# Half of the second group's w_in part by 20 products, and the sums of w_in moved to GpSimd

## The chip, the cores and the metric

The kernel runs on one core of a Trainium2 chip. The metric is the device time of one execution in microseconds (us); lower is better. The core has five engines with a queue each: TensorE (matmul; PE in the profile, and PEld for its weight loads), VectorE (DVE), ScalarE (ACT), GpSimd (POOL) and SyncE (SP, which issues most of the DMAs here).

## The reference

```python
def _attn_ref(q, k, v, alpha):                      # (4, 8, 768, 48) each
    for t in range(S):
        state = alpha[:, :, t, :, None] * state + einsum('bhd,bhe->bhde', k[:, :, t], v[:, :, t])
        y[:, :, t] = einsum('bhd,bhde->bhe', q[:, :, t], state)
def _moe_ref(x, w_in, w_out):                       # x (3072, 384), w_in (384, 2048), w_out (2048, 384)
    h = x @ w_in
    g = h * (1.0 / (1.0 + exp(-h)))
    return g @ w_out
```

A gated linear recurrence over 768 steps, for 4 batches of 8 heads of width 48, gives 3072 rows of 384 numbers (x). They go through a matrix of 384 x 2048 (w_in), the silu function, and a matrix of 2048 x 384 (w_out).

## The kernel before

The rows are cut into 24 chunks of 128 tokens. The recurrence of a chunk is done in stages spread over the steps of the main loop (from line 1357): products and quotient (L766, L795: scans on VectorE), scores (L834: matmuls, copies by ScalarE and a causal select by GpSimd, L860 for the first 8 chunks and L872 after them), values and states (L898, L924). Between the stages the loop puts pieces of the two big matrix products, as filler for TensorE.

Four chunks make a group, so there are 6 groups (grp 0 to 5). A group's 512 rows are two halves h of 256 columns in `xt`. The 2048 columns of w_in are cut into two pairs (pair 0 and 1) of 1024, and a pair into 2 tiles of 4 x 128 columns. A group's work on w_in can be done in two ways:

- `enter_plain(grp, h, pair)` (L971): 4 pieces, each 2 x 3 matmuls of 128x128 weights by 256 columns, and one silu by ScalarE (L983). A group and pair need it for both h: 8 pieces, 48 matmuls.
- `enter(grp, pair)` (L991): a fast matrix multiplication with 20 products in place of 24, each for the 2 tiles of the pair: 7 pieces, 40 matmuls. It needs sums of blocks of x (`sums_x`, L950, 11 sums, in the tile `xc`) and sums of blocks of w_in (`sums_w`, L608, 23 sums for each pair, in the tile `wx` and over blocks of w_in itself, so that plain work on that pair can't follow). It evicts its PSUM banks by copies of ScalarE (L1010) and additions and subtractions of VectorE (L1018), before four silus by ScalarE (L1015).

All sums are made by `combine` on VectorE (L599 to L606): an addition, a subtraction, or, where both signs are negative, one scalar_tensor_tensor. In `SUMS_W` two of the 23 have both signs negative (the 10th and the 17th).

`leave(grp, h)` (L1111) is the work on w_out for half a group: 7 pieces, one product of 8 matmuls each, after a scheme with 7 products in place of 8. Between them VectorE subtracts cells of g (L1123), and the four results are copied (L1130) or added (L1132) into `o` (3 buffers) and stored by a DMA on GpSimd's queue (L1135). After each piece `done()` (L1140) issues up to four sums of w_in: those of pair 0 in leave(0, 1), those of pair 1 in leave(1, 0).

The order of the pieces is written out by hand (L1225 to L1244): plain work for all of group 0 and for (grp 1, h 0, pair 0); leave(0, 0); plain (1, 1, 0); then leave(0, 1) interleaved piece by piece with the plain work of group 1 on pair 1; then leave(1, 0) with enter(2, 0), leave(1, 1) with enter(2, 1), and so on. Each piece has a weight of 12 (0 for sums of x), and `fill` (L1275) issues pieces so that a phase is done by its mark. `settle` (L1262) runs once in between: it closes the staging pools of the first phase, makes the later tiles (`xc` and `wx` among them), clears three load buffers by GpSimd memsets (L1272) and loads chunk 8.

The queue of an engine is filled by a scheduler, in the order in which instructions come ready. `tc.keep_in_program_order` pins an instruction behind the one traced before it on its engine; all sums of w_in are pinned.

Of the kernel before, what the change touches and what calls it, by code (L numbers as in the profile page):

```python
# [356 lines left out]
def quotients(  # L357
# [61 lines left out]
    def pool(name, bufs=1, space=None):  # L419
        kw = {} if space is None else {"space": space}  # L420
        return ctx.enter_context(tc.tile_pool(name=name, bufs=bufs, **kw))
# [169 lines left out]

    quads = w_in.rearrange("p k (q i c) -> p i k q c", i=4, c=128)

    def block_w(at):

        return quads[:, at // NKT, at % NKT] if at < 4 * NKT else late["wx"][:, at - 4 * NKT]


    def combine(to, sa, a, sb, b):  # L599
        if sa == sb == 1:  # L600
            return dve.tensor_tensor(to, a, b, ALU.add)
        if sa == 1:
            return dve.tensor_tensor(to, a, b, ALU.subtract)
        if sb == 1:
            return dve.tensor_tensor(to, b, a, ALU.subtract)
        return dve.scalar_tensor_tensor(to, a, -1.0, b, ALU.mult, ALU.subtract)  # L606

    def sums_w(pair, upto):  # L608

        r = slice(2 * pair, 2 * pair + 2)  # L610
        while sums_done[pair] < min(upto, len(SUMS_W)):
            to, sa, a, sb, b = SUMS_W[sums_done[pair]]
            tc.keep_in_program_order(
                combine(block_w(to)[:, r], sa, block_w(a)[:, r], sb, block_w(b)[:, r]))
            sums_done[pair] += 1

    sums_done = [0] * (NQ // 2)
# [326 lines left out]
    def block_x(grp, at):  # L944

        if at < 2 * NKT:
            return xts[2 * grp + at % 2][:, at // 2, :]
        return xcs[grp][:, at - 2 * NKT, :]

    def sums_x(grp):  # L950
        xcs[grp] = late["xc"]
        for i, (to, sa, a, sb, b) in enumerate(SUMS_X):
            if i == 2:
                yield
            tc.keep_in_program_order(
                combine(block_x(grp, to), sa, block_x(grp, a), sb, block_x(grp, b)))
        yield
# [33 lines left out]
    def enter(grp, pair):  # L991
        g_tiles(grp, pair)
        halves = [gts[grp, h, pair] for h in range(2)]

        s = [halves[o % 2][:, o // 2] for o in range(8)]
        todo = iter(PRODUCTS)

        def new(i):
            return bank(i).rearrange("p (e n) -> p e n", e=2)

        def add(ps, first=False):
            w, x = next(todo)
            for e in range(2):
                pe.matmul(ps[:, e], lhsT=block_w(w)[:, 2 * pair + e], rhs=block_x(grp, x),
                          start=(first and e == 0), stop=(e == 1), skip_group_check=True)

        def copy(ps, to=None):
            if to is None:
                to = late["part"].tile([128, 2, TB], F32, name="part")
            act.copy(to, ps)  # L1010
            return to

        def silu(h, i):
            x = halves[h][:, i : i + 2]
            return act.activation(x, x, AF.Silu)  # L1015

        def tt(to, a, b, op=ALU.add):
            dve.tensor_tensor(to, a, b, op)  # L1018

        a, b, c = [new(i) for i in range(3)]  # L1020
        add(a, True)
        copy(a, s[6])
        add(b, True)
        copy(b, s[2])
        add(c, True)
        tt(s[6], s[6], copy(c), ALU.subtract)
        yield
        add(c)
        copy(c, s[7])
        add(b)  # L1030
        copy(b, s[4])
        add(a)
        tt(s[7], s[7], copy(a), ALU.subtract)
        yield
        add(a)
        copy(a, s[5])
        add(b)
        copy(b, s[3])
        tt(s[5], s[5], s[3])
        add(c)  # L1040
        copy(c, s[0])
        yield
        add(a)
        tt(s[4], a, s[4])
        b = new(1)
        add(b, True)
        add(b)
        copy(b, s[1])
        yield
        c = new(2)  # L1050
        add(c, True)
        t = copy(c)
        late_2 = (grp, pair) == (4, 0)
        if not late_2:
# [12 lines left out]
        yield  # L1067
        add(c)
        tt(s[1], c, s[1])
        late_3 = (grp, pair) in ((2, 0), (4, 0))  # L1070
        if not late_3:
            tt(s[3], s[1], s[3], ALU.subtract)
        a = new(0)
        add(a, True)
        tt(s[2], a, s[2])
        if late_3:
            tt(s[3], s[1], s[3], ALU.subtract)
        add(b)
        tt(s[7], b, s[7])
        silu(1, 2)  # L1080
        yield
        add(c)
        total = combine(s[1], -1, s[1], -1, s[0])
        if late_2:
            tc.keep_in_program_order(total)
        tt(s[0], c, s[0])
        silu(0, 0)
        a = new(0)
        add(a, True)
        tt(s[3], a, s[3])  # L1090
        silu(1, 0)
        turn.append(turn.pop(0))
        for h in range(2):
            side_by_side(grp, h, pair)
        yield
# [15 lines left out]
    def leave(grp, h):  # L1111
# [28 lines left out]
        def done():  # L1140
            at = next(passed)
            if grp == h == 0 and at in (2, 3):
                other_differences(at - 2)
            if 2 * grp + h in (1, 2):
                sums_w(2 * grp + h - 1, 4 * next(steps) + 4)

        alone = grp == h == 0 or grp == NG - 1
        a, b = out_bank(0, HO), out_bank(1, HO)
# [63 lines left out]
    def plain(grp, h, pair):  # L1212
        return (enter_plain(grp, h, pair), 12, 2 * (2 * grp + h) + 2)
# [7 lines left out]
    def both(x, y):  # L1221
        for i in range(max(len(x), len(y))):
            pieces.extend(x[i : i + 1] + y[i : i + 1])
# [4 lines left out]
            pieces += [plain(0, h, pair)] * 4  # L1228
    pieces += [plain(1, 0, 0)] * 4 + [(leave(0, 0), 12, GB)] * 7
    phases = [len(pieces)]  # L1230
    pieces += [plain(1, 1, 0)] * 4
    both([(leave(0, 1), 12, GB)] * 7, [plain(1, 0, 1)] * 4 + [plain(1, 1, 1)] * 4)
    phases.append(len(pieces))
    before = output(1)
    for grp in range(2, NG):
# [26 lines left out]
    def settle():  # L1262

        first.close()
        late.update(look=pool("look"), part=pool("part"), turn=pool("turn"),
                    xc=pool("xc").tile([128, len(SUMS_X), TB], F32, name="xc"),
                    wx=pool("wx").tile([128, 8, NQ, 128], F32, name="wx"))
        quads = pool("quads")
        late["p"] = pool("p").tile([128, NP * W + 1], F32, name="p")
        late["quads"] = {name: quads.tile([128, 32 + 4 * NP * D], F32, name=f"{name}t") for name in "akq"}  # L1270
        for name, t in late["quads"].items():
            gps.memset(t, 1.0 if name == "a" else 0.0)  # L1272
        load(NA)
# [191 lines left out]
```

## Time and profile before

| what | value |
|---|---|
| median of 3 runs | 550.11 us (549.88 to 550.41) |
| the profiled execution | 549.8 us, its span 548.1 us |
| TensorE busy | 538.7 us, 98% of the span |
| VectorE busy | 432.8 us, 79% |
| ScalarE busy | 216.3 us, 39% |
| GpSimd busy | 79.4 us, 14% |
| granted TensorE clock | 0.999 |

The span runs from the first instruction to the last. Times within it are given from its start. The first piece of leave(0, 0) starts at 97.7 us, the four pieces of plain (1, 1, 0) run from 122.3 us, leave(0, 1) starts at 135.9 us, and the phase of leave(1, 0) and enter(2, 0) at 184.6 us. In a row of a timeline stand start and length in us, engine, line, operation, what it writes and reads, shape and count, and in brackets the idle time before it with what ended it.

### The profile page before, as it was taken

Reading aid. Unit: us, or ns where it says so; the run is one execution under the profiler, and the core shown is the slowest. Engines: PE = TensorE matmul, PEld = TensorE weight load, DVE = VectorE, ACT = ScalarE, POOL = GpSimd, SP = SyncE. Lnnn points to the kernel's source line nnn. Section 1 sums busy time; section 2 is a strip of 40 time slices with the busy share of each in tenths; the row PEclk is TensorE's granted clock in tenths of the full one; section 3 lists DMA queues with packets and bytes.
Section 4 is the critical chain, followed back from the end, with each engine's and each line's share of the span. In section 5 each row is a group of like instructions: output and inputs, shape, how many; then the busy total and the mean of one; then the engine's idle time right before and its main releaser. Section 6 shows DMA issues by size and latency. Waiting matters only on the chain.

```text
span 548.1 us, 12704 instructions
## 1 busy us (share of the span) xinstructions
PE 538.7 (98%) x5069; PEld 493.1 (90%) x5069; DVE 432.8 (79%) x753; ACT 216.3 (39%) x490; POOL 79.4 (14%) x146
## 2 busy tenths in 40 slices
PE   8899999999999999999999999999999999999996
PEld 8788888998999899899999999998998999999996
DVE  5999789986979799996998986998884796944421
ACT  3655554223333334444444354253264342432200
POOL 4111001131212201111121021021121000001000
PEclk9999999999999999999999999999999999999999
DMA  9999861355445434445455653716742144500001
GB/s 213 301 203 248 220 188 33 94 147 139 111 120 134 122 84 119 122 138 159 123 132 146 186 134 98 212 28 167 192 126 85 54 129 148 166 9 19 12 22 35
DMA packets 99219, 70.12 MB, mean 128 GB/s; under 512 B 56272, under 2 KB 88656, under 8 KB 99152
## 3 DMA queue, kind: packets, MB, share of 16 engines
q1 hardware_dynamic: 97232, 65.30, 46.0%
q0 software_dynamic: 1920, 3.93, 2.1%
q8 instruction: 41, 0.67, 0.5%
q14 instruction: 26, 0.21, 0.1%
HBM read 61.34 MB, written 7.86 MB: 126 GB/s over the span
## 4 chain that ended last, share of the span: by engine, by line
PE 96%; DVE 1%; issue 1%; POOL 0%; ACT 0%; DVEq 0%; ACTq 0%; POOLq 0%
PE ps_m L395 45%; PE ps_o L395 38%; PE ps_a L395 12%; PE ps_a L399 2%; DVE p L805 0%; DVE u L775 0%; PE ps_o L399 0%; POOL g L860 0%; DVE p L812 0%; DVE kp L786 0%; ACT xt L923 0%; ACT g L859 0%; ACT al L764 0%; DVE least L778 0%; ACT o L1130 0%
## 5 line engine op out<-in xcount | busy, mean ns | idle before, releaser
L395 PE MATMUL ps_o<-w_out,g 128*128 128x192 f32 x720 | 125.6, 328 | 0.0
L395 PEld LDWEIGHTS ps_o<-w_out,g 128*128 128x128 f32 x720 | 117.8, 190 | 2.7 <-issue 0.4
L395 PE MATMUL ps_m<-xt,w_in 128*128 128x256 f32 x480 | 111.6, 381 | 0.5 <-ACT xt L923 0.5
L395 PEld LDWEIGHTS ps_m<-xt,w_in 128*128 128x128 f32 x480 | 89.9, 190 | 12.7 <-ACT xt L923 0.8
L395 PE MATMUL ps_o<-wt,g 128*128 128x192 f32 x528 | 91.4, 326 | 0.0
L395 PEld LDWEIGHTS ps_o<-wt,g 128*128 128x128 f32 x528 | 87.3, 190 | 1.7 <-DVE o L1132 0.3
L395 PE MATMUL ps_m<-xc,w_in 128*128 128x256 f32 x288 | 70.6, 381 | 0.0
L1123 DVE TENSOR_TENSOR g<-g 128x512 f32<-128x512 f32 x72 | 49.6, 702 | 14.6 <-PE ps_o L395 12.2
L872 POOL TENSOR_SCALAR_AFFINE_SELECT g<-g 64x256 f32<-64x256 f32 x64 | 36.0, 563 | 165.3 <-ACT g L865 162.1
L395 PEld LDWEIGHTS ps_m<-xc,w_in 128*128 128x128 f32 x288 | 53.7, 190 | 6.7
L1015 ACT ACTIVATE g<-g 128x1024 f32<-128x1024 f32 x32 | 33.2, 1057 | 55.5 <-DVE g L1018 55.5
L1010 ACT COPY g<-ps_m 128x512 f32<-128x512 f32 x64 | 37.0, 587 | 36.7 <-PE ps_m L395 36.6
L395 PE MATMUL ps_m<-xc,wx 128*128 128x256 f32 x192 | 50.1, 383 | 0.0
L1135 POOL DMA_DIRECT2D out_dram<-o x40 | 22.1, 552 | 169.9 <-ACT o L1130 74.9
L1018 DVE TENSOR_TENSOR g<-ps_m,g 128x512 f32<-128x512 f32 x56 | 37.5, 684 | 10.9 <-PE ps_m L395 10.5
L395 PEld LDWEIGHTS ps_m<-xc,wx 128*128 128x128 f32 x192 | 35.2, 190 | 4.1 <-issue 0.4
L775 DVE TENSOR_TENSOR_SCAN u<-al,one 128x516 f32<-128x516 f32 x24 | 29.7, 1236 | 7.0 <-ACT al L764 6.6
L983 ACT ACTIVATE g<-ps_m 128x512 f32<-128x512 f32 x32 | 19.0, 597 | 33.2 <-PE ps_m L395 32.9
L805 DVE TENSOR_TENSOR_SCAN p<-al,inv 128x516 f32<-128x516 f32 x24 | 29.8, 1243 | 2.0 <-PE ps_a L395 1.1
L728 DVE TENSOR_REDUCE seen<-bits 128x1 f32<-128x512 int32 (+1 forms) x33 | 26.2, 820 | 6.0 <-DMA bits<-in_moe_w_in_dram 6.0
L1010 ACT COPY part<-ps_m 128x512 f32<-128x512 f32 x32 | 18.9, 590 | 30.4 <-PE ps_m L395 20.4
L1132 DVE TENSOR_TENSOR o<-ps_o,u 128x192 f32<-128x192 f32 x21 | 7.4, 353 | 26.9 <-PE ps_o L395 11.8
(142 smaller groups left out, 681.4 us busy)
## 6 DMA issues: line engine op xcount, KB each, us to landing
bits<-in_moe_w_in_dram SPq DMA_DIRECT2D x24, 512.0 KB, 5.1
bits<-in_moe_w_out_dram SPq DMA_DIRECT2D x16, 384.0 KB, 3.9
at<-in_alpha_dram SPq DMA_DIRECT2D x64, 96.0 KB, 2.6
kt<-in_k_dram SPq DMA_DIRECT2D x64, 96.0 KB, 2.7
qt<-in_q_dram SPq DMA_DIRECT2D x64, 96.0 KB, 2.8
bits<-in_alpha_dram SPq DMA_DIRECT2D x9, 512.0 KB, 4.0
out_dram<-o POOLq DMA_DIRECT2D x40, 96.0 KB, 2.2
flips<-turn SPq DMA_DIRECT2D x12, 256.0 KB, 2.4
```

What stands on the lines that cost most here:

```text
L395: in_order(nc.tensor.matmul(*args, **kw))
L399: in_order(nc.tensor.transpose(*args))
L728: dve.tensor_reduce(seen[kind][which][:, i : i + 1], x, axis=AX, op=op, apply_absolute_value=True))
L775: settled(dve.tensor_tensor_scan(u[:, end - 1 :: -1], sg[:, end:0:-1], one[:, end:0:-1], 0.0, ALU.mult, ALU.add))
L805: settled(dve.tensor_tensor_scan(p[:, 0:end], sg[:, 0:end], iv[:, 0:end], 0.0, ALU.mult, ALU.add))
L872: gps.affine_select(x, x, pattern=[[0, NP], [1, CH]], compare_op=ALU.is_ge, fill=0.0, base=0, channel_multiplier=-1)
L983: settled(act.activation(gts[grp, h, pair][:, i : i + 2, q % 2, :], ps, AF.Silu))
L1010: act.copy(to, ps)
L1015: return act.activation(x, x, AF.Silu)
L1018: dve.tensor_tensor(to, a, b, op)
L1123: dve.tensor_tensor(cells(grp, h, pair, *to), cells(grp, h, pair, *x), cells(grp, h, pair, *y), ALU.subtract)
L1135: (gps if grp < NG - 1 else nc.sync).dma_start(out[r : r + C, c * HO : (c + 1) * HO], o)
```

## The change

The work of group 1 on pair 1 is done by `enter(1, 1)` (20 products) in place of eight pieces of plain work. For that, the sums of x for group 1 are made after plain (1, 1, 0), and the sums of w_in for pair 1 come earlier: in leave(0, 0) in place of leave(1, 0). Those of pair 0 stay in leave(0, 1). All sums of w_in are handed to GpSimd, except the two of each pair with both signs negative, for which `combine` still takes VectorE. The tile `wx` becomes two, one for each pair; that of pair 1 is made in the pool `fix` at the start, that of pair 0 in `settle`.

```diff
-    def block_w(at):
-        return quads[:, at // NKT, at % NKT] if at < 4 * NKT else late["wx"][:, at - 4 * NKT]
+    wx = [None, fix.tile([128, 8, 2, 128], F32, name="wx1")]
+    def block_w(at, pair):
+        return quads[:, at // NKT, at % NKT, 2 * pair : 2 * pair + 2] if at < 4 * NKT else (
+            wx[pair][:, at - 4 * NKT])
...
-    def combine(to, sa, a, sb, b):
+    def combine(to, sa, a, sb, b, eng=dve):
         if sa == sb == 1:
-            return dve.tensor_tensor(to, a, b, ALU.add)
+            return eng.tensor_tensor(to, a, b, ALU.add)
         if sa == 1:
-            return dve.tensor_tensor(to, a, b, ALU.subtract)
+            return eng.tensor_tensor(to, a, b, ALU.subtract)
         if sb == 1:
-            return dve.tensor_tensor(to, b, a, ALU.subtract)
+            return eng.tensor_tensor(to, b, a, ALU.subtract)
         return dve.scalar_tensor_tensor(to, a, -1.0, b, ALU.mult, ALU.subtract)
...
-                combine(block_w(to)[:, r], sa, block_w(a)[:, r], sb, block_w(b)[:, r]))
+                combine(block_w(to, pair), sa, block_w(a, pair), sb, block_w(b, pair), gps))
...
-                pe.matmul(ps[:, e], lhsT=block_w(w)[:, 2 * pair + e], rhs=block_x(grp, x),
+                pe.matmul(ps[:, e], lhsT=block_w(w, pair)[:, e], rhs=block_x(grp, x),
...
-            if 2 * grp + h in (1, 2):
-                sums_w(2 * grp + h - 1, 4 * next(steps) + 4)
+            if grp == 0:
+                sums_w(1 - h, 4 * next(steps) + 4)
...
-    pieces += [plain(1, 1, 0)] * 4
-    both([(leave(0, 1), 12, GB)] * 7, [plain(1, 0, 1)] * 4 + [plain(1, 1, 1)] * 4)
+    sums = sums_x(1)
+    pieces += [plain(1, 1, 0)] * 4 + [(sums, 0, 2 * GB)] * 2
+    both(output(0)[1], group(1)[1])
...
-                    xc=pool("xc").tile([128, len(SUMS_X), TB], F32, name="xc"),
-                    wx=pool("wx").tile([128, 8, NQ, 128], F32, name="wx"))
+                    xc=pool("xc").tile([128, len(SUMS_X), TB], F32, name="xc"))
+        wx[0] = pool("wx").tile([128, 8, 2, 128], F32, name="wx0")
```

More of the change, by code (lines that the diff above doesn't have):

```diff
@@ L592, in quotients @@
     quads = w_in.rearrange("p k (q i c) -> p i k q c", i=4, c=128)
-    def block_w(at):
-        return quads[:, at // NKT, at % NKT] if at < 4 * NKT else late["wx"][:, at - 4 * NKT]
-    def combine(to, sa, a, sb, b):
+    wx = [None, fix.tile([128, 8, 2, 128], F32, name="wx1")]
[3 more added lines that the diff above has]
+    def combine(to, sa, a, sb, b, eng=dve):
         if sa == sb == 1:
-            return dve.tensor_tensor(to, a, b, ALU.add)
+            return eng.tensor_tensor(to, a, b, ALU.add)
         if sa == 1:
-            return dve.tensor_tensor(to, a, b, ALU.subtract)
+            return eng.tensor_tensor(to, a, b, ALU.subtract)
         if sb == 1:
-            return dve.tensor_tensor(to, b, a, ALU.subtract)
+            return eng.tensor_tensor(to, b, a, ALU.subtract)
         return dve.scalar_tensor_tensor(to, a, -1.0, b, ALU.mult, ALU.subtract)
     def sums_w(pair, upto):
-        r = slice(2 * pair, 2 * pair + 2)
         while sums_done[pair] < min(upto, len(SUMS_W)):
```

## The prediction

> **What bounds the kernel now.** I read the chain of waits first, then the busy time by windows around the parts that change, then the timelines of TensorE, VectorE and GpSimd through the first w_out part.
>
> ```profile
> PE 96%; DVE 1%; issue 1%; POOL 0%; ACT 0%; DVEq 0%; ACTq 0%; POOLq 0%
> ```
> ```profile
> 97.70:122.30 24.60, 24.37 (x311) 23.37 (x308) 21.04 (x35) 5.16 (x14) 7.63 (x11) 1.00 0.47 121
> 122.30:135.90 13.60, 13.57 (x168) 11.64 (x168) 9.46 (x14) 5.14 (x15) 1.65 (x4) 1.00 0.55 141
> 135.90:188.20 52.30, 52.30 (x627) 47.53 (x617) 44.47 (x83) 16.12 (x48) 9.96 (x16) 1.00 0.47 122
> 188.20:230.30 42.10, 42.10 (x436) 38.42 (x432) 41.61 (x77) 18.39 (x43) 6.48 (x12) 1.00 0.38 100
> ```
>
> A windows row gives the stretch, its length, then busy us of TensorE, its weight loads, VectorE, ScalarE, GpSimd, then the granted clock. The rows are: leave(0, 0); the 4 pieces of plain(1, 1, 0); leave(0, 1) with the second half of w_in of group 1; the first half of the next phase. TensorE is 96% of the chain and busy all through three of the rows, at clock 1.00. So TensorE work that goes away is time gained, one for one, and VectorE work that goes away is not: in the last row VectorE is busy 41.61 of 42.10 us and TensorE still loses nothing.
>
> **The saving.** One piece of plain work is 2 x 3 matmuls in the code and 12 in the trace, so each counts twice there:
>
> ```profile
> 139.55 2.86 PE L395 MATMUL ps_m<-xt,w_in 128*128 128x256 f32 x12
> ```
> ```profile
> 177.43 5.18 PE ps_m L395 x24
> ```
>
> The second row is the chain's: 24 matmuls in 5.18 us, 0.216 us each. Removed: 8 pieces of 12, 96 matmuls. Added: 20 products x 2 columns of tiles x 2, 80. So 16 x 0.216 = **3.46 us less TensorE**, whatever else happens.
>
> **VectorE and ScalarE.** Of 2 x 23 sums, two per half have both signs negative and stay on VectorE, so 42 leave it for GpSimd. The fourth window loses its 23 altogether (2 of them to the first window); TensorE is already full there, so that buys nothing. In the second and third windows VectorE loses 21 sums and gains 11 sums of x and the 14 additions of enter():
>
> ```profile
> L601 DVE TENSOR_TENSOR xc<-xt x12: 383/419/427, 178.0 to 436.3; 128x256 f32<-128x256 f32 x12
> ```
> ```profile
> L603 DVE TENSOR_TENSOR wx<-w_in x4: 418/521/624, 142.0 to 199.0; 128x256 f32<-128x256 f32 x4
> ```
> ```profile
> L1018 DVE TENSOR_TENSOR g<-ps_m,g 128x512 f32<-128x512 f32 x56 | 37.5, 684 | 10.9 <-PE ps_m L395 10.5
> ```
>
> Durations are min/median/max in the first two. 9.46 + 44.47 = 53.9 us now; less 21 x 0.42 = 8.8; plus 11 x 0.42 = 4.6; plus 14 x 0.684 = 9.6: 59.3 us, in 65.9 - 3.5 = 62.4 us. It fits with 3.1 us over, if nothing slows it. ScalarE trades 8 silus for copies and 4 wider silus; at 16.12 of 52.30 us it covers that: zero, or a few us on TensorE if a bank copy came late behind another ScalarE step. That wx1 lies in memory of its own from the start removes a wait on released memory; it costs nothing in time.
>
> **GpSimd's sums, the disputed cost.** No GpSimd addition of two tensors is in the trace. What is there is GpSimd's select, which reads one tensor, and what VectorE does beside it:
>
> ```profile
> 80.31 1.23 POOL L860 TENSOR_SCALAR_AFFINE_SELECT g<-g 128x512 f32<-128x512 f32 x2 [16.88 <-ACT g L859]
> 94.11 1.62 POOL L860 TENSOR_SCALAR_AFFINE_SELECT g<-g 128x512 f32<-128x512 f32 x2 [12.58 <-ACT g L859]
> 102.92 0.77 POOL L1272 MEMSET at<- 128x800 f32 x1 [7.19 <-ACT xt L923]
> ...
> 109.81 2.53 POOL L860 TENSOR_SCALAR_AFFINE_SELECT g<-g 128x512 f32<-128x512 f32 x2 [4.72 <-ACT g L859]
> ```
> ```profile
> 94.25 0.99 DVE L624 TENSOR_TENSOR wt<-w_out 128x384 f32<-128x384 f32 x1
> 95.16 1.45 DVE L625 TENSOR_TENSOR wt<-w_out,wt 128x384 f32<-128x384 f32 x2
> 96.53 0.55 DVE L634 TENSOR_TENSOR w_out<-w_out 128x384 f32<-128x384 f32 x1
> 97.00 0.55 DVE L627 TENSOR_TENSOR wt<-w_out,wt 128x384 f32<-128x384 f32 x1
> 97.47 0.55 DVE L624 TENSOR_TENSOR wt<-w_out 128x384 f32<-128x384 f32 x1
> 98.05 0.56 DVE L625 TENSOR_TENSOR wt<-w_out,wt 128x384 f32<-128x384 f32 x1
> 98.53 0.69 DVE L1106 TENSOR_TENSOR g<-g 128x512 f32<-128x512 f32 x1
> 99.13 1.23 DVE L775 TENSOR_TENSOR_SCAN u<-al,one 128x516 f32<-128x516 f32 x1
> 100.39 0.17 DVE L778 TENSOR_SCALAR least<-u 128x4 f32<-128x4 f32 x1
> 100.59 0.69 DVE L786 TENSOR_TENSOR kp<-ps_a,u 128x512 f32<-128x512 f32 x1
> 101.20 0.17 DVE L803 RECIPROCAL inv<-least 128x4 f32<-128x4 f32 x1
> 101.41 1.23 DVE L805 TENSOR_TENSOR_SCAN p<-al,inv 128x516 f32<-128x516 f32 x1
> 102.56 0.67 DVE L1123 TENSOR_TENSOR g<-g 128x512 f32<-128x512 f32 x1
> ...
> 108.48 1.12 DVE L739 STREAM_TRANSPOSE al<-at 128x512 f32<-128x512 f32 x1 [1.17 <-DMA at<-in_alpha_dram]
> ...
> 113.76 0.67 DVE L1123 TENSOR_TENSOR g<-g 128x512 f32<-128x512 f32 x1
> ```
>
> The same L624 takes 0.55 us alone and 0.99 us while the selects of 94.11 run: an operation of VectorE with two inputs in SBUF waits while GpSimd reads 512 elements a partition, 0.44 us; and the pair of selects takes 1.62 us in place of 1.23. Beside the smaller selects (256 elements) a sum of L603 goes from 418 to at most 624 ns, 0.21 us. A sum on GpSimd reads 2 x 256 = 512 elements, so I take **0.44 us for each VectorE operation that it meets**; the ends are 0.21 (both inputs read at once) and 0.61 (half of the undisturbed 1.23: VectorE shut out for the whole operation). The sum itself then lasts between VectorE's own 0.42 and about 0.55 + 0.44 = 1.0 us; 0.61 alone is the nearest row.
>
> [...]
>
> **Where that lands: leave(0, 0).** The first sum is pinned behind GpSimd's previous instruction, the select that ends at 95.73, and GpSimd idles 7.19 us from there. So 11 sums (4, 4, and 3 with one on VectorE) start at 95.73, where VectorE has no idle row until 108.48. Between 95.73 and the first L1123 stand eight operations with two SBUF inputs that can meet a sum: L634, L627, L624, L625, L1106, L775, L805, and L1123 itself. 8 x 0.44 = 3.5 us late. That L1123 makes the weights for the second product of leave(0, 0):
>
> ```profile
> 105.06 2.63 PEld L395 LDWEIGHTS ps_o<-wt,g 128*128 128x128 f32 x16
> ...
> 114.54 2.63 PEld L395 LDWEIGHTS ps_m<-w_out,g 128*128 128x128 f32 x16
> ```
>
> It is done at 102.56 + 0.67 = 103.23, 1.83 us ahead of 105.06. So TensorE stalls 3.5 - 1.8 = **1.7 us** (ends: 8 x 0.21 = 1.7, no stall; 8 x 0.61 = 4.9, 3.1 us).
>
> Behind GpSimd's sums queue also: the memsets, the selects of the next scores, and the four output DMAs.
>
> ```profile
> 112.92 0.69 POOL L1135 DMA_DIRECT2D out_dram<-o  x1 [0.58 <-ACT o L1130]
> ...
> 119.99 1.08 PE L395 MATMUL ps_a<-g,vn 128*32 128x128 f32 x32
> ...
> 120.75 0.54 POOL L1135 DMA_DIRECT2D out_dram<-o  x1 [1.99 <-ACT o L1130]
> ```
>
> The selects of 109.81 end at 112.34 and feed the products of 119.99: 7.6 us, which covers 4 sums of 1.0 us. Each output DMA waits behind up to 4 sums, 2.4 to 4.0 us; there are three o buffers, the fourth store comes 7.8 us after the first, and 3.8 us are left for that transfer: zero. The first sum left on VectorE waits for GpSimd's ninth; behind it in VectorE's queue stands the transpose of 108.48, which idles 1.17 us anyway. The second comes after the third output product and can hold up VectorE by a sum, 1.0 us, ahead of work for the next chunk: zero to TensorE. The memset rival below is where this cover is gone.
>
> **Sum.** Against the profiled execution (549.8 us, span 548.1): 549.8 - 3.46 + 1.7 = 548.0. The median of the runs is 0.3 higher, so **548.4 us**; its own range, for one more or one fewer meeting and for small stalls in the later phase, is 547.3 to 549.4.
>
> **Rivals.**
>
> *No stall.* If the two inputs cost only 0.21 us, 1.7 us of delay fits in 1.8 us of lead: 550.11 - 3.46 = 546.65. For it: the small selects; and in the last window a VectorE at 99% costs TensorE nothing. Against: L624's 0.44.
>
> *The memsets.* The memsets of the load buffers stand behind the 11 sums. At up to 1.0 us each these end at 107, not before 102.9, and the loads of chunk 8 with them 4.1 us later; L739 at 108.48 already idles for that DMA. Less the 1.7 us that TensorE has lost too, VectorE is 2.4 us late there, and two more meetings add 0.9. The L1123 of 113.76 ends at 114.43; the second half of the product of 114.54 needs it at 114.54 + 1.3 = 115.84. 2.4 + 0.9 - 1.4 = 1.9 us more: 550.3, no change. Against: with sums of 0.61 us, 11 end at 102.4 and nothing is late; and a scheduler that foresees the late load may put that L1123 ahead.
>
> *A lock for the whole operation.* VectorE is held 0.61 us by each sum, 3.1 us of stall: 549.8, no change. [...]
>
> *VectorE becomes the bound (slower).* Place: leave(0, 1) with enter(1, 1). VectorE has 59.3 of 62.4 us there before any meeting. Each of the 21 sums that meets one costs 0.44; from 7 meetings on, VectorE has more work than time. All 21: 9.2 us, 6.1 too much; half: 1.5 too much. TensorE would wait for the evictions of its banks that enter() gives to VectorE. The middle, 3.8 us, on top of the first stall: 552.2. For it: in this stretch VectorE also waits at times for others, so 62.4 us are not all usable. Against: the next phase gives back 23 x 0.42 = 9.7 us of VectorE, and the last window shows that TensorE bears a full VectorE.
>
> **How the numbers follow.** Forecast 0.30, no stall 0.20, memsets 0.18, whole lock 0.10, VectorE bound 0.22. A measurement of this kernel tells 0.2% (1.1 us) from no change: faster is below 549.0, slower above 551.2. Faster: 0.20 + 0.27 of the forecast = 0.47. Same: 0.03 of the forecast, 0.13 of the memsets, 0.07 of the lock = 0.23. Slower: 0.22, and 0.05 and 0.03 where those two come with a late VectorE, = 0.30. The range takes in the case without a stall and the middle of the VectorE case: 546.4 to 552.4.
>
> **What would show it.** The saving: 16 fewer matmuls in ps_m groups (1008 for 1024). The price: GpSimd additions of 128x256, 0.6 to 1.0 us each, the first at about 95.8; L634 to L1123 between 96 and 107 lengthened by 0.44 each. The stall: a gap of TensorE ahead of the second ps_o<-wt product, released by L1123. Wrong if that gap is missing or above 3 us; if GpSimd's additions last well over 1 us; or if gaps of TensorE stand in the enter(1, 1) stretch, released by L1018.

## The result and the profile after

The changed kernel takes **556.44 us** (median of 4, 555.96 to 558.33) against 550.0 (549.65 to 550.41) before: ratio 1.0123, 95% interval 1.0099 to 1.0148. It is **slower**, by 6.4 us by the medians and 6.8 by the ratio; the forecast was 548.4, its range 546.4 to 552.4. The profiled execution has a span of 554.2 us and a mean granted clock of 0.996.

Busy time and, below the dots, the chain that ended last, from the page of the kernel after:

```profile
PE 539.0 (97%) x5053; PEld 491.1 (89%) x5053; DVE 442.7 (80%) x736; ACT 221.6 (40%) x498; POOL 114.2 (21%) x188
...
PE 70%; DVE 18%; DMA 4%; ACT 2%; issue 2%; SPq 2%; POOL 0%; DVEq 0%; ACTq 0%; POOLq 0%
```

TensorE has its 16 instructions less (5053; before 5069), and its share of the chain fell from 96% to 70%. VectorE has 18% where it had 1%. Its busy time grew by 9.9 us. 42 sums left it (18.5 us before), and the 14 additions of enter and 11 sums of x came (some 14 us, an estimate from the durations before), so some 14 us are operations that became longer.

Two windows of the kernel after, leave(0, 0) and leave(0, 1) with enter(1, 1), cut at the same products as those shown of before:

```profile
97.96:128.08 30.12, 26.47 (x311) 24.85 (x308) 28.21 (x39) 5.15 (x14) 22.20 (x27) 0.94 0.34 88
...
141.65:193.08 51.43, 48.69 (x580) 43.53 (x568) 49.55 (x76) 21.22 (x54) 25.44 (x33) 1.00 0.42 110
```

Leave(0, 0) takes 30.12 us in place of 24.60, with TensorE idle for 3.65 of them and a granted clock of 0.94. The next stretch is only 0.87 us shorter (51.43 for 52.30), where 3.46 us of matmuls went: TensorE idles 2.74 us in it.

**The stall.** VectorE beside GpSimd's first sums, timelines of the kernel after (lines are two higher than before, so L1108 is the old L1106, L788 the old L786):

```profile
95.43 1.98 DVE L627 TENSOR_TENSOR wt<-w_out,wt 128x384 f32<-128x384 f32 x2
...
97.34 1.08 DVE L636 TENSOR_TENSOR w_out<-w_out 128x384 f32<-128x384 f32 x1
...
99.34 1.08 DVE L626 TENSOR_TENSOR wt<-w_out 128x384 f32<-128x384 f32 x1
...
101.34 1.22 DVE L1108 TENSOR_TENSOR g<-g 128x512 f32<-128x512 f32 x1
102.49 1.75 DVE L777 TENSOR_TENSOR_SCAN u<-al,one 128x516 f32<-128x516 f32 x1
104.28 0.51 DVE L780 TENSOR_SCALAR least<-u 128x4 f32<-128x4 f32 x1
104.81 0.69 DVE L788 TENSOR_TENSOR kp<-ps_a,u 128x512 f32<-128x512 f32 x1
...
107.14 1.15 DVE L1125 TENSOR_TENSOR g<-g 128x512 f32<-128x512 f32 x1
```
```profile
97.07 0.93 POOL L606 TENSOR_TENSOR wx<-w_in,wx 128x256 f32<-128x256 f32 x1
...
104.72 0.72 POOL L608 TENSOR_TENSOR w_in<-wx,w_in 128x256 f32<-128x256 f32 x1
```

The operations of 0.55 us take 1.08, L1108 1.22 for 0.69, the scan 1.75 for 1.23, the pair at 95.43 1.98 for 1.45: about **0.53 us more each**. One `wt` operation (0.41) and the scan of p (0.36) lost less. kp, which reads a PSUM tile, takes its 0.69 as before. A GpSimd sum takes 0.72 us where nothing meets it (104.72, beside kp) and 0.93 and more where something does.

TensorE at that place, before and after:

```profile
101.40 0.84 PE L395 MATMUL ps_a<-p,st 128*32 128x128 f32 x24
102.06 0.52 PE L395 MATMUL ps_a<-vn,kn 128*32 128x48 f32 x32
102.51 2.87 PE L395 MATMUL ps_m<-wt,g 128*128 128x192 f32 x16
```
```profile
101.66 0.84 PE L395 MATMUL ps_a<-p,st 128*32 128x128 f32 x24
105.56 0.66 PE L395 MATMUL ps_a<-vn,kn 128*32 128x48 f32 x32 [3.06 <-DVE kp L788]
106.15 4.38 PE L395 MATMUL ps_m<-wt,g 128*128 128x192 f32 x16
```

The states product waits for kp, by the trace. It does not read kp (it reads vn and kn): it writes a `ps_a` bank, of which the kernel has three, and the one whose turn it is holds the input of kp until VectorE has read it. So what comes late is the release of a bank. Before, kp ended at 100.59 + 0.69 = 101.28, and the product began at 102.06: a lead of 0.78 us. After, kp ends at 105.50, 4.2 us later, and TensorE stands 3.06 us. Then the product `ps_m<-wt` takes 4.38 us for 2.87. The reason is in the windows of the kernel after:

```profile
103.00:106.00 3.00, 0.44 (x32) 0.44 (x32) 2.90 (x5) 0.04 (x1) 2.92 (x4) 0.97 0.00 0
106.00:109.00 3.00, 3.00 (x21) 2.88 (x13) 3.00 (x4) 0.00 (x0) 2.92 (x4) 0.50 0.35 59
```

The granted clock is 0.50 for 3.4 us behind the gap (105.8 to 109.3). The second loss, in the stretch of enter(1, 1), is spread, as TensorE's waits in the kernel after show (total, times, longest):

```profile
PE ps_a L395 <- DVE kp L788: 3.1, 1, 3.1
...
PE ps_a L395 <- DVE p L814: 1.3, 3, 0.6
PE ps_o L395 <- ACT g L1017: 0.8, 1, 0.8
PE ps_o L395 <- DVE o L1134: 0.8, 2, 0.4
...
PE ps_m L395 <- DVE g L1020: 0.5, 1, 0.5
```

### The profile page after: what moved, and what is told of

Same layout as the page of the kernel before. It is cut to its first block, busy times and chain, and to the rows that moved or that the text cites. A ratio compares the mean times of both kernels' runs of the same rounds, so it can differ in the third digit from the quotient of the medians.

```text
span 554.2 us, 12693 instructions
## 1 busy us (share of the span) xinstructions
PE 539.0 (97%) x5053; PEld 491.1 (89%) x5053; DVE 442.7 (80%) x736; ACT 221.6 (40%) x498; POOL 114.2 (21%) x188
## 4 chain that ended last, share of the span: by engine, by line
PE 70%; DVE 18%; DMA 4%; ACT 2%; issue 2%; SPq 2%; POOL 0%; DVEq 0%; ACTq 0%; POOLq 0%
PE ps_m L395 31%; PE ps_o L395 31%; PE ps_a L395 7%; DVE u L777 2%; DVE p L807 2%; SPq L505 1%; DVE turn L741 1%; DVE w_out L679 1%; DVE w_out L680 1%; DVE g L1125 1%; DMA flips<-turn 1%; DVE xc L604 1%; DVE p L814 1%; DVE al L741 1%; DMA at<-in_alpha_dram 1%
## 5 line engine op out<-in xcount | busy, mean ns | idle before, releaser
L395 PE MATMUL ps_m<-xt,w_in 128*128 128x256 f32 x396 | 92.9, 381 | 0.8 <-ACT xt L925 0.5
L395 PEld LDWEIGHTS ps_m<-xt,w_in 128*128 128x128 f32 x396 | 74.0, 190 | 11.6 <-DVE w_in L680 1.1
L395 PE MATMUL ps_m<-xc,w_in 128*128 128x256 f32 x324 | 79.7, 382 | 0.1
L395 PEld LDWEIGHTS ps_m<-xc,w_in 128*128 128x128 f32 x324 | 60.3, 190 | 8.0 <-ACT part L1012 0.4
L1017 ACT ACTIVATE g<-g 128x1024 f32<-128x1024 f32 x36 | 37.5, 1057 | 60.8 <-DVE g L1020 60.7
L1012 ACT COPY g<-ps_m 128x512 f32<-128x512 f32 x72 | 41.5, 586 | 41.6 <-PE ps_m L395 41.5
L395 PE MATMUL ps_m<-xc,wx 128*128 128x256 f32 x216 | 56.3, 383 | 0.0
L1020 DVE TENSOR_TENSOR g<-ps_m,g 128x512 f32<-128x512 f32 x63 | 42.2, 683 | 11.2 <-PE ps_m L395 10.7
L395 PEld LDWEIGHTS ps_m<-xc,wx 128*128 128x128 f32 x216 | 39.6, 190 | 4.5 <-issue 0.4
L862 POOL TENSOR_SCALAR_AFFINE_SELECT g<-g 128x512 f32<-128x512 f32 x16 | 11.8, 760 | 85.1 <-ACT g L861 85.1
```

The costliest lines, as they stand in the source:

```text
L395: in_order(nc.tensor.matmul(*args, **kw))
L862: gps.affine_select(g[:, u], g[:, u], pattern=[[0, NP], [1, C]], compare_op=ALU.is_ge, fill=0.0, base=0, channel_multiplier=-1)
```

## The experiments

The theory after this reading: a GpSimd sum costs VectorE 0.53 us for each operation with two SBUF inputs that it meets; VectorE has leads of 0.8 to 3.5 us at the places looked at, and where a lead is used up TensorE stands, and after a stand of 3.06 us its clock was at half for 3.4 us. The rivals: VectorE simply has too much work of its own in the new order; or the loss comes from the moved loads, memsets and memory.

**1. The same sums, made by VectorE.**

```diff
-                combine(block_w(to, pair), sa, block_w(a, pair), sb, block_w(b, pair), gps))
+                combine(block_w(to, pair), sa, block_w(a, pair), sb, block_w(b, pair), dve))
```

> All sums of w_in made by VectorE, in the places that the change gives them. Theory (meetings): GpSimd's reads hold up VectorE's operations with two inputs by about 0.5 us each, so the sums cost more on GpSimd than the 0.42 us that they take on VectorE, and there the scheduler can put them behind what is urgent. Then the 3.06 us gap ahead of the states of chunk 6 is gone, with the stretch at clock 0.5; VectorE is over full in both leave(0, 0) and enter(1, 1), so other gaps remain: 551 to 554 us, faster than the changed kernel. Rival (work): VectorE's load is what counts and GpSimd takes it off; then 42 more sums of 0.42 us make it worse: 558 to 565 us.

Measured: 557.12 us, ratio 1.0136 (1.0119 to 1.0153). TensorE in it, and the window behind its longest gap:

```profile
122.04 4.16 PE L395 MATMUL ps_o<-wt,g 128*128 128x192 f32 x16 [2.67 <-DVE o L1134]
```
```profile
123.00:126.00 3.00, 3.00 (x12) 2.69 (x10) 2.97 (x7) 0.00 (x0) 0.54 (x1) 0.58 0.26 89
```

The gap behind kp is gone, and another of 2.67 us stands at 119.4 behind an addition into `o`, with the half clock after it. The time lies between the two forecasts, so neither had it: work of 0.42 us a sum costs this order as much as meetings of 0.53, and VectorE has room for neither in it.

**2. The first sums take GpSimd's time, but read nothing.** Each pair 1 sum becomes three memsets of its target; these sums are left out.

```diff
+            if pair == 1 and not sa == sb == -1:
+                for _ in range(2):
+                    tc.keep_in_program_order(gps.memset(block_w(to, pair), 0.0))
...
+                gps.memset(block_w(to, pair), 0.0) if pair == 1 and not sa == sb == -1 else
```

> Each of the 21 GpSimd sums of pair 1 (those in leave(0, 0)) is left out and three memsets of the same block stand in its place, so that GpSimd is about as long busy but reads nothing; half of the hidden columns of groups 1 to 5 are wrong by that. Theory (meetings): a memset holds up nothing on VectorE; the gap ahead of the states of chunk 6 and the stretch at clock 0.5 are gone, the later stalls stay: 556.4 - 5.2 = 551.2 us. Rival (queue): what counts is how long GpSimd's queue is held up, since the memsets of the load buffers, the selects and the output DMAs stand behind the sums: 555 to 556 us still.

Measured: 551.19 us, ratio 1.0029 (1.0019 to 1.0038). VectorE and GpSimd at the place of the stall:

```profile
96.65 0.55 DVE L633 TENSOR_TENSOR wt<-w_out,wt 128x384 f32<-128x384 f32 x1
97.12 0.55 DVE L630 TENSOR_TENSOR wt<-w_out 128x384 f32<-128x384 f32 x1
```
```profile
96.31 0.68 POOL L617 MEMSET wx<- 128x256 f32 x2
97.05 0.31 POOL L619 MEMSET wx<- 128x256 f32 x1
```

GpSimd is about as busy as with sums, the memsets of the load buffers come late here too (105.07 to 107.25; before from 102.92), and VectorE's operations have their 0.55 us again; TensorE has no gap in leave(0, 0). So it is the reading of SBUF (1.08 us beside sums, 0.55 beside memsets), not GpSimd's queue. In the change the two engines take turns: a sum ends at 99.00, VectorE's operation at 99.42, and so on with about 1.00 us to a turn. VectorE loses 0.53 of the 0.72 us that a sum's record lasts; that it is held for all of it is not shown.

**3. No sum reads anything.** All 42 GpSimd sums become one memset each (all left out).

```diff
+                gps.memset(block_w(to, pair), 0.0) if True and not sa == sb == -1 else
```

> The kernel after, with each of the 42 GpSimd sums of w_in replaced by one memset of its target: GpSimd still has its queue entries, reads nothing, and is busy for less; the sums of the hidden columns of groups 1 to 5 are left out, so the time is that of the same kernel without any meeting of a GpSimd read with VectorE. With pair 1 alone made into memsets the kernel took 551.2 us, TensorE losing about 4.6 us in leave(0, 1) with enter(1, 1) and the phase after, against the 3.46 us it is spared. Theory A (that loss is VectorE being held up by the pair 0 sums, about 10 to 12 meetings of 0.53 us): most of it goes, 547 to 548 us, 549.9 - 3.46 + 0.5 to 1.5, and the gaps of ps_m behind L1018 to L1025 and ps_a behind p shrink below 0.5 us each. Theory B (the sums of x, the additions of enter and the copies already fill VectorE and ScalarE there; meetings cost little): it stays at 550.5 to 551.5 us with the same gaps.

Measured: 547.89 us, ratio 0.9965 (0.9953 to 0.9978): faster than before by 1.9 us. Without the sums, which it cannot do without, the new order would pay. Of the 3.46 us, 1.5 are not gained. TensorE has small waits from 170 us on that it did not have before, for L1021 (0.4 us), for an addition into `o` (0.4) and for a copy of ScalarE (0.2). They make 1.0 us, and the profiled execution, the fastest with 547.34 us, lost no more; what the slower ones lost besides is not shown. And the stretch shows how thin the lead is. The step p of a chunk on VectorE (first fence: the kernel without sums, then before), and TensorE's product that waits for it:

```profile
151.59 0.69 DVE L815 TENSOR_TENSOR p<-turn,p 128x512 f32<-128x512 f32 x1
```
```profile
154.60 0.90 PE L395 MATMUL ps_a<-p,kp 48*64 48x128 f32 x32
```
```profile
150.71 0.69 DVE L812 TENSOR_TENSOR p<-turn,p 128x512 f32<-128x512 f32 x1
```
```profile
154.93 0.90 PE L395 MATMUL ps_a<-p,kp 48*64 48x128 f32 x32
```

Before, p had ended 3.5 us ahead (154.93 - 151.40); with enter's additions and sums of x, 2.3 us ahead. The pair 0 sums use that up: in the kernel of experiment 2, where they are the only ones, the product waits.

```profile
155.77 0.90 PE L395 MATMUL ps_a<-p,kp 48*64 48x128 f32 x32 [0.82 <-DVE p L818]
```

**4. The other half.** Only the pair 0 sums are memsets (left out); the pair 1 sums stay.

```diff
+                gps.memset(block_w(to, pair), 0.0) if pair == 0 and not sa == sb == -1 else
```

> The kernel after with only the pair 0 sums on GpSimd replaced by one memset each; the pair 1 sums in leave(0, 0) stay as they are. The sums of one half of the hidden columns are left out. Without any sum it took 547.9 us, with the pair 0 sums alone 551.2, with both 556.4. Theory (two separate losses that add): 547.9 + 556.4 - 551.2 = 553.1, range 552.6 to 553.7 us, with the 3.1 us gap behind kp and the half clock, and no gap of over 0.7 us after 140 us. Rival (VectorE's lateness of leave(0, 0) is carried into the later stretch and makes part of the loss there): 551 to 552.3 us or above 554.3.

Measured: 553.41 us, ratio 1.0057 (1.0042 to 1.0073), as the theory had it. TensorE's longest wait in it:

```profile
PE ps_a L395 <- DVE kp L789: 3.1, 1, 3.1
```

In parts of the time before: without sums 0.9965; pair 0's sums add 1.0029 - 0.9965 = 0.0064 (3.5 us), pair 1's 1.0057 - 0.9965 = 0.0092 (5.1 us). Together 1.0121, and the change has 1.0123. By the intervals each loss is known to about 1 us; so far they add, and together they are what the change loses against experiment 3. For pair 1's loss the trace has the gap of 3.1 us and a fall of the clock (mean 0.994), which at the 3.4 us of the kernel after takes half of that: 4.8 by this estimate. For pair 0's, TensorE idles 2.9 us from 140 to 190 us in experiment 2 and 0.8 in experiment 3; some 1.4 of the 3.5 us are not placed.

**5. The kernel before, with additions that nobody needs.** 11 additions of GpSimd where the change has its first sums; nothing else is changed.

```diff
+    scrap = fix.tile([128, 2, 128], F32, name="scrap")
...
+            for i in range((4, 4, 3)[at] if grp == h == 0 and at < 3 else 0):
+                tc.keep_in_program_order(gps.tensor_tensor(
+                    scrap, quads[:, i, 0, 2:4], quads[:, i, 1, 2:4], ALU.add))
```

> The kernel before, with only 11 useless GpSimd additions of 128x256 added (they read blocks of w_in and write a tile that nothing reads) after the first three pieces of leave(0, 0): 4, 4 and 3, where the change puts its first sums. No product is left out, nothing else is moved. Theory (the meetings of these additions with VectorE make kp late, TensorE stands about 3 us at the states product, and its clock then is at half for 3.4 us): 549.9 + 3.1 + 1.6 to 2.2 = 554.6 to 555.2 us, with VectorE's operations at 96 to 107 us longer by 0.53 each and the granted clock 0.5 in one row of three us behind the gap. Rival (the gap comes from something else of the change, as the moved loads or the memory): 549.5 to 550.5 us.

Measured: 554.3 us, ratio 1.0076 (1.0055 to 1.0098). VectorE, TensorE and the window behind the gap:

```profile
97.09 1.08 DVE L635 TENSOR_TENSOR w_out<-w_out 128x384 f32<-128x384 f32 x1
...
102.24 1.75 DVE L776 TENSOR_TENSOR_SCAN u<-al,one 128x516 f32<-128x516 f32 x1
```
```profile
105.31 0.87 PE L395 MATMUL ps_a<-vn,kn 128*32 128x48 f32 x32 [3.14 <-DVE kp L787]
106.11 3.91 PE L395 MATMUL ps_m<-wt,g 128*128 128x192 f32 x16
```
```profile
106.00:109.00 3.00, 3.00 (x23) 2.89 (x12) 3.00 (x5) 0.00 (x0) 2.92 (x4) 0.62 0.37 64
```

Additions alone make the same lengthened operations, the same gap behind kp and the same fall of the clock. Of the four executions three took 554.0 to 554.8 us at a mean clock of 0.994 to 0.997, and one 553.0 at 1.000: by that the fall of the clock is worth 1 to 1.8 us and does not come every time.

**6 and 7. Fewer of them.** Four additions, and six; the edit against experiment 5:

```diff
-            for i in range((4, 4, 3)[at] if grp == h == 0 and at < 3 else 0):
+            for i in range((4, 0, 0)[at] if grp == h == 0 and at < 3 else 0):   # four
+            for i in range((4, 2, 0)[at] if grp == h == 0 and at < 3 else 0):   # six
```

> The kernel before with only 4 useless GpSimd additions of 128x256 after the first piece of leave(0, 0); with 11 it took 554.3 us: TensorE stood 3.1 us at the states product behind kp and then ran 3.4 us at a lower clock. Theory (each VectorE operation with two SBUF inputs that meets an addition is 0.53 us longer, kp has a lead of 0.7 us, and the clock falls only after a long gap): four additions end at about 100.0 us and meet four or five of VectorE's operations before kp, 2.0 to 2.4 us late, gap 1.3 to 1.7 us, no fall of the clock: 551.2 to 551.6 us. Rival 1 (the clock falls after any gap of over 1 us): 552.8 to 553.3 us. Rival 2 (the additions are hidden until the memsets and loads are late, which only 11 of them make): 549.5 to 550.3 us.

> The kernel before with 6 useless GpSimd additions of 128x256, 4 after the first piece of leave(0, 0) and 2 after the second. Theory as with four: six end at about 102 us and meet six or seven operations before kp, 3.0 to 3.5 us late, gap 2.3 to 2.8 us: 552.2 to 552.7 us if the clock holds after a gap of that length, 553.8 to 554.3 us if it falls. The longest gap without a fall seen so far is 1.8 us, the shortest with one 2.67 us: this run narrows that. Rival (the loss does not grow with the number of additions): the same time as with four, within 0.4 us.

Measured: 550.91 us with four, ratio 1.0021 (1.0012 to 1.003), and 552.39 with six, ratio 1.0044 (1.0031 to 1.0058). TensorE with four, then with six, and the window with six:

```profile
103.70 0.55 PE L395 MATMUL ps_a<-vn,kn 128*32 128x48 f32 x32 [1.25 <-DVE kp L787]
104.18 2.87 PE L395 MATMUL ps_m<-wt,g 128*128 128x192 f32 x16
```
```profile
104.81 0.55 PE L395 MATMUL ps_a<-vn,kn 128*32 128x48 f32 x32 [2.28 <-DVE kp L787]
105.29 4.55 PE L395 MATMUL ps_m<-wt,g 128*128 128x192 f32 x16
```
```profile
106.00:109.00 3.00, 3.00 (x12) 3.00 (x11) 2.96 (x7) 0.00 (x0) 2.17 (x3) 0.55 0.53 98
```

The gap grows by half a microsecond for each addition (1.25 with four, 2.28 with six) and stops growing once kp is past: 11 make 3.14. With four, the clock holds (1.00 in each window from 97 to 112 us), the product takes 2.87 us, and the time is the gap and no more (1.2 us by the ratio). With six, the fall does not come every time: one of five executions, the profiled one, took 553.7 us at a mean clock of 0.995, the other four 551.6 to 553.0 at 1.000. The expectation had 552.2 to 552.7 if the clock holds and 553.8 to 554.3 if it falls; both came, to within 0.6 us.

**8. No gap: TensorE kept busy by useless matmuls.** 14 products with the identity ahead of the states product.

```diff
+            if n == 6:
+                dummy = banks[2].tile([128, 512], F32, name="ps_m")
+                for _ in range(14):
+                    tc.keep_in_program_order(
+                        nc.tensor.matmul(dummy[:, 0:C], lhsT=ident, rhs=ident, start=True, stop=True))
```

> The changed kernel with 14 matmuls of no use (identity times identity into a free bank, about 3.1 us) ahead of the states of chunk 6, where TensorE waits 3.06 us. Theory (clock): the idle time itself makes the granted clock fall to 0.5 for 3.4 us, which costs 1.5 to 1.7 us on top of the gap; with TensorE busy through the wait the clock stays at 1.0: 554.8 us, and the products after it take 2.87 us and not 4.38. Rival: the clock does not follow the gap, or the products are slow for another reason: 556.4 us or later.

Measured: 563.22 us, ratio 1.0237 (1.022 to 1.0254). TensorE in it, and the window behind the useless products:

```profile
101.90 3.39 PE L935 MATMUL ps_m<-ident 128*128 128x128 f32 x28
...
105.70 2.87 PE L395 MATMUL ps_m<-wt,g 128*128 128x192 f32 x16
...
121.44 4.47 PE L395 MATMUL ps_m<-w_out,g 128*128 128x192 f32 x16 [3.40 <-DVE g L1130]
```
```profile
106.00:109.00 3.00, 3.00 (x20) 3.00 (x19) 3.00 (x5) 0.32 (x1) 3.00 (x4) 1.00 0.00 0
```

At the place itself it went as expected: VectorE was as late, the clock stayed at 1.00, and the product took 2.87 us. But the scheduler put SP's loads in another order, the alpha load of the next chunk came late (VectorE waits 3.00 us for it, until 115.32), and two new gaps hide the gain: 3.40 us, with the clock at 0.50 from 123 to 126 us behind it, and 2.94 us, where the `ps_o<-wt` products behind it take 4.31 us for 2.87. As a measure of the whole it is inconclusive.

**9. The first sums later.** Two after each of the last three pieces of leave(0, 0), five after each piece of plain (1, 1, 0).

```diff
+            if grp == h == 1:
+                sums_w(1, 6 + 5 * (f // 2 + 1))
...
-            if grp == 0:
-                sums_w(1 - h, 4 * next(steps) + 4)
+            if grp == 0 and h == 1:
+                sums_w(0, 4 * next(steps) + 4)
+            if grp == h == 0 and at >= 4:
+                sums_w(1, 2 * (at - 3))
```

> The change, with the sums of pair 1 moved behind the full stretch of VectorE: 2 after each of the last pieces of leave(0, 0) from the fifth on, 5 after each piece of plain (1, 1, 0), where VectorE was busy 9.46 of 13.6 us. Theory (meetings): the first gap and the low clock go, 5.2 us back, at most 1 us of new stalls: 551 to 552.5 us; what is left over 546.7 is the enter(1, 1) stretch. Rival (the half by products is too much for VectorE wherever the sums stand): the stall moves to the next stretch, 555 to 557 us.

Measured: 556.86 us, ratio 1.0124 (1.0107 to 1.0141). VectorE and TensorE in it:

```profile
126.89 0.93 DVE L609 SCALAR_TENSOR_TENSOR wx<-w_in,wx 128x256 f32<-128x256 f32 x1 [5.67 <-POOL w_in L608]
```
```profile
156.65 3.10 PE L395 MATMUL ps_m<-xc,w_in 128*128 128x256 f32 x8 [2.79 <-ACT part L1014]
```

The gap behind kp is gone. The sum with both signs negative, left on VectorE, now waits 5.67 us for GpSimd's sum before it, with all of VectorE's work behind it, and TensorE's gap has moved to 156 us, behind a copy of ScalarE. The rival's time came.

**10. The same, and no sum on VectorE.** In the tables of sums (of w_in and of x) some blocks are stored with the other sign, so that no sum of w_in has both signs negative.

```diff
-    (6, -1, 2, 1, 18), (18, -1, 11, -1, 18), (7, 1, 7, -1, 8), (5, -1, 3, 1, 7),
+    (6, -1, 2, 1, 18), (18, 1, 11, 1, 18), (7, 1, 7, -1, 8), (5, -1, 3, 1, 7),
...
-    (9, -1, 18, -1, 9), (4, 1, 16, 1, 5), (4, 1, 13, 1, 4), (1, 1, 1, -1, 2),
-    (1, -1, 0, 1, 1), (8, 1, 15, 1, 18), (8, 1, 17, 1, 8),
+    (9, 1, 18, -1, 9), (4, 1, 16, 1, 5), (4, 1, 13, 1, 4), (1, 1, 1, -1, 2),
+    (1, -1, 0, 1, 1), (8, 1, 15, -1, 18), (8, 1, 17, 1, 8),
...
-    (11, 1, 5, -1, 10), (12, 1, 4, 1, 11), (15, -1, 0, 1, 12), (16, 1, 1, -1, 15),
+    (11, 1, 5, -1, 10), (12, 1, 4, 1, 11), (15, 1, 0, -1, 12), (16, 1, 1, 1, 15),
```

> The kernel with the pair 1 sums spread later (2 after each of the last three pieces of leave(0, 0), 5 after each piece of plain(1, 1, 0)), which took 556.9 us, and in addition the sign table rewritten so that no sum has both signs negative: none of w_in's sums is left on VectorE. What is computed stays the same. Theory (the 5.7 us for which VectorE stood at the sum left on it, waiting for GpSimd's sum before it, held up the sums of x and all behind): that wait is gone, the gap of 2.79 us at 156.65 and the half clock of 3.4 us after it with it, so 556.9 - 2.8 - 1.7 = 552.4, range 551 to 553.5 us. Rival (VectorE was the bound there by its work and its meetings, the wait was idle time it could spare): 555.5 to 557 us, and the gap moves to another wait for VectorE.

Measured: 559.01 us, ratio 1.0171 (1.0154 to 1.0187). TensorE in it:

```profile
160.25 1.38 PE L395 MATMUL ps_a<-p,kp 48*64 48x128 f32 x32 [4.97 <-DVE p L814]
```

My theory fell here: the wait of 5.67 us went, and the time grew, beyond the rival's 555.5 to 557 too. GpSimd is now busy for 3.7 to 3.9 of every 4 us from 120 to 156, VectorE for 3.9 to 4.0 from 136 on, and p, which had 2.3 us of lead in this stretch without sums, is 5 us late for TensorE.

**11 and 12. Spread further.** Both keep the tables of experiment 10. First, on top of experiment 10, 12 of pair 0's sums on GpSimd in leave(0, 1), and the last 11 on VectorE in leave(1, 0), in the phase after. Then pair 1's too, mostly half by half on VectorE and GpSimd, in the places where VectorE stood idle in experiment 3.

```diff
+            if grp == 0 and h == 1:
+                sums_w(0, min(2 * at + 2, 12))
+            if grp == 1 and h == 0:
+                sums_w(0, (17, 20, 23)[min(at, 2)], dve)
```
```diff
+            if grp == h == 1:
+                sums_w(1, 4 * (f // 2 % 4) + 10, dve)
+                sums_w(1, 4 * (f // 2 % 4) + 12)
...
+            if grp == 0 and h == 1:
+                sums_w(0, 3 * max(at - 1, 0))
+            if grp == 1 and h == 0:
+                sums_w(0, (18, 21, 23)[min(at, 2)], dve)
+            if grp == h == 0 and at >= 3:
+                sums_w(1, 2 * (at - 2))
```

> The kernel with no sum on VectorE of the run before this one, and the pair 0 sums split: 12 of 23 stay on GpSimd in leave(0, 1) (2 after each piece), 11 are made by VectorE after the first three pieces of leave(1, 0), in the next phase, where VectorE lost 23 sums to the change. Theory (the stretch of leave(0, 1) with enter(1, 1) is bound by VectorE, and each sum that meets it there costs 0.53 us): 11 fewer meetings there, most of the loss of about 4.6 us against the saving goes, 549 to 551 us. Rival (the additions and sums of x of enter alone fill VectorE there, or the 11 sums late in the next phase hold up its first products): 551.5 to 554 us.

> A version that spreads all the sums over the places where VectorE stands idle in the run without sums (106 to 112, 128 to 134 and 158 to 164 us), with no sum of both signs negative: pair 1, 2 on GpSimd after each of the last four pieces of leave(0, 0), then 2 on VectorE and 2 on GpSimd after each piece of plain(1, 1, 0); pair 0, 3 on GpSimd after each of the last five pieces of leave(0, 1) and the last 8 on VectorE in the first three pieces of leave(1, 0). Theory (what costs time is VectorE held up while it is the bound, between 134 and 158 us above all): no gap of 2.5 us or more, so no half clock, small gaps of 2 to 3 us in all beside the saving of 3.46: 549.0 to 550.5 us. Rival (VectorE has no room anywhere in that stretch, and the work comes late wherever it is put): 552 to 556 us with a gap of over 2.5 us before 165 us.

Measured: 556.77 us, ratio 1.0137 (1.0112 to 1.0161), and 555.48, ratio 1.0115 (1.0094 to 1.0137). TensorE in the first, then in the second:

```profile
158.83 0.90 PE L395 MATMUL ps_a<-p,kp 48*64 48x128 f32 x32 [2.67 <-DVE p L814]
```
```profile
157.85 0.90 PE L395 MATMUL ps_a<-p,kp 48*64 48x128 f32 x32 [2.39 <-DVE p L814]
```

The rivals were right in what they name: it is the product behind p each time. The first kernel is slower than its rival's 551.5 to 554 us; the second lies in its rival's range, with a gap of 2.39 us where over 2.5 was expected. There is a further gap of 1.5 to 1.6 us in the next phase, where VectorE made the last sums. In the second kernel the window behind the gap has the clock at 1.00:

```profile
159.00:162.00 3.00, 3.00 (x19) 2.95 (x18) 2.97 (x4) 2.72 (x11) 2.24 (x4) 1.00 0.75 172
```

Of the orders tried none comes near the kernel before, and none is told from the change except experiment 10, which is slower. That the 20 products would pay if the sums cost nothing (experiment 3) is shown; a place for the sums was not found, and whether there is one stays open.

## Why the prediction was wrong, point by point

- **The saving** held: 1008 matmuls in ps_m groups for 1024, 16 x 0.216 = 3.46 us. So did the reading that VectorE work taken away gains nothing.
- **The price of a meeting** was near: 0.53 us measured, 0.44 taken, ends 0.21 and 0.61. The sums lasted 0.72 to 1.5 us, 0.6 to 1.0 expected. By price alone this is 0.7 us over 8 meetings.
- **The step that failed first: "It is done at 102.56 + 0.67 = 103.23, 1.83 us ahead of 105.06. So TensorE stalls 3.5 - 1.8 = 1.7 us".** It names the wrong wait. That L1123 ended 5.1 us late (107.14 + 1.15 = 108.29), and nothing waited for it: its product, the third of leave(0, 0) by the timeline and not the second, began at 110.37. TensorE already stood at the states product, which needs the bank that kp frees, 0.78 us after kp's end. kp stood in the list I quoted, but I looked only for what TensorE reads of VectorE, not for what VectorE must have read. The delay was short as well: of the eight operations six come up to kp, 6 x 0.44 = 2.6 us, which with kp's lead would be a stall of 1.9. kp was 4.2 us late: some 0.09 more for each of the six, 0.53 for the `wt` operation ahead of my list, 0.34 for `least`, and 0.26 because the whole stretch began later. The gap I said would prove me wrong "above 3 us" came at 3.06, and ahead of another product.
- **The missing term: the clock.** The sum counted a stall at its length. A stall of 3.06 us brought 3.4 us at half clock behind it: `ps_m<-wt` took 4.38 us for 2.87. The granted clock was 1.00 in every row that I showed, and I took it as given.
- Together these make leave(0, 0) dearer by 5.1 us (experiment 4) and not 1.7.
- **The step that cost most: "It fits with 3.1 us over, if nothing slows it".** By it the forecast put the stretch of enter(1, 1) at nothing. VectorE as the bound there was a rival at 0.22 with 3.8 us, and it happened as well: 3.5 us for pair 0's sums and 1.5 that were missing without them, 5.0 of the 8.0 us between forecast and measurement. The total did fit (VectorE is busy 59.8 of 65.0 us in the two windows of after); but a total says nothing of one result's lead: that of p fell from 3.5 us to 2.3 by the work, and below zero by the meetings. The waits named L1018 (now L1020) for 0.5 us, but p for 1.3.
- **Zero for the sums left on VectorE**: no wait of TensorE in the change is put down to them, but as a rule it is wrong: moved later, the same sum held VectorE up for 5.67 us.
- **The memsets** came at 107.68 as that rival said. No cost of theirs can be told: with them at 105.07 to 107.25 and no reads (experiment 2), TensorE had no gap in leave(0, 0); at 107.68 they were not tried alone.
- **No stall** and **a lock for the whole operation** fell with the price: 0.53 lies between their 0.21 and 0.61. That the lock's stall, 3.1 us, is the length of the gap that came is luck: it was worked out for L1123 and by a count of meetings that did not hold for kp.

The forecast took one of two losses for likely and the other for a rival. They exclude each other in no way: 550.0 - 3.46 + 1.5 + 3.5 + 5.1 = 556.6, and 556.44 was measured. The 1.5 us are what experiment 3 left over, so what this sum tests is that the two halves add up to the whole.

## What to carry to other kernels

When an engine that is off the path is to be delayed, list everything of it that the bound engine waits for in that stretch, the results that are read and the buffers that have to be freed, with the end of the one and the start of the other, and set the delay against the smallest lead; the sum of busy time over the stretch says nothing about it. A GpSimd operation that reads SBUF is not free for VectorE: here each sum handed over cost VectorE 0.53 us where it met something, and VectorE makes it in 0.42. And a stall of TensorE cost up to 1.7 us more than its length here, half of 3.4 us at a clock of 0.50: no gap of up to 1.60 us did that, one of 2.28 us did, and one of 2.39 us did not.

## What the hardware showed unexpectedly

**The granted clock falls to half behind some gaps of TensorE.** The profiled executions had gaps of 2.28, 2.67, 2.67, 2.79, 2.94, 3.06, 3.1, 3.14, 3.40 and 4.97 us with a lower clock behind them, and one of 2.39 us (experiment 12) with the clock at 1.00. For seven of the ten the windows give the clock, and where a window of 3 us lies within the fall (the kernel after, experiment 8) it is 0.50. Behind 2.79 and 2.94 us the length of the products shows it (3.10 us for 1.99, 4.31 for 2.87), and for the 3.1 us of experiment 4 the page does, with the clock below 0.9 in its slice from 97 to 111 us. Gaps of 1.00 to 1.60 us did not have it. In the six traces whose windows cover a whole fall (the kernel after and experiments 1, 5, 7, 10 and 11) the clock lost in it makes 1.68 to 1.72 us, which is 3.4 us at 0.50. A gap of 2.28 us brought a fall and one of 2.39 us none, so the length of the gap alone does not decide; what does is not shown.

And the same kernel can go both ways. By the mean clock of each execution, the clock fell with six additions in one of five (0.995; the others 1.000) and with eleven in three of four (0.994 to 0.997; the other 1.000). That is indirect: three executions of the kernel before, too, had a mean clock of 0.995 and took about 1 us longer than the others.

**A GpSimd addition of 128x256 lasts 0.72 us and takes 0.53 from a VectorE operation with two SBUF inputs** (1.08 us for 0.55), and itself becomes longer by up to 0.8 us (0.72 to 1.53). A memset beside the same operations costs them nothing (0.55 us). `least`, an operation with one small input, also became longer: 0.17 us alone, 0.32 beside a memset, 0.51 beside an addition. Both times it ended within 0.05 us of the GpSimd operation beside it.
